# Windowed attention with its keys on the partitions and two heads in one matmul, in front of a routed expert layer

## The chip, the cores and the metric

The kernel runs on one core of one Trainium2 chip. The metric is the device time of that core in microseconds (us), taken over several runs; the profile shows one execution of the same program. A core has TensorE (matmuls, PE in the profile, with its weight loads as PEld), VectorE (DVE), ScalarE (ACT), GpSimd (POOL) and SyncE (SP, which here only issues transfers). All of the data is float32.

## The reference

Eight sequences of 576 tokens go through attention with 8 heads of 64 dimensions, in which a query sees itself and the 63 keys before it. The 512 numbers of a token then go to one of eight experts, which is chosen token by token: a token either picks the expert with its largest logit, or takes over the expert of the token before it.

```python
scores = scale * np.matmul(q, k.transpose(0, 1, 3, 2))       # scale = 1 / 8
mask = (rel >= 0) & (rel < window)                           # rel = query - key, window = 64
scores = np.where(mask, scores, -1000000000.0)
scores = scores - np.max(scores, axis=-1, keepdims=True)
attn = np.exp(scores)
attn = attn / (np.sum(attn, axis=-1, keepdims=True) + 1e-09)
x = np.matmul(attn, v)                                       # then (B, S, H * D)
...
logits = np.einsum('bsd,de->bse', x, w_gate)                 # 8 experts
local_gate = 1.0 / (1.0 + np.exp(-np.einsum('bsd,de->bse', x, w_local).squeeze(-1)))
...
h = np.maximum(x[b, s] @ w1[e], 0.0)
out[b, s] = p[e] * (h @ w2[e])                               # e: fresh argmax, or the token before's; p = softmax of logits
```

The queries, keys and values are normal random numbers times 0.1.

## The kernel before

Three functions follow one another. `attention` writes the attention's rows to DRAM (`xs`) and the nine gate columns of each token to SBUF (`lt`). `route` works out from `lt` which expert each token has, and sorts the tokens into 25 blocks of 256 places, each with one expert. `experts` takes a block at a time: it gathers 256 rows of x, transposes them (L432), multiplies with the expert's first matrix (L440, 128x256 tiles), then with its second (L452, 128x512 tiles), and scatters the rows of the output (L456). It needs the routing's result for each of its fetches, so nothing of it runs beside the attention.

`attention` walks over 36 chunks of 128 tokens, in two halves of four heads. The queries are on the partitions of a score tile. `scores` (L127) makes 128 queries against 192 keys, one head a matmul; two heads lie on the two halves of the 128 partitions, so that each matmul uses 64 rows of TensorE. VectorE scales and adds the mask (L137; L133 in the chunks that have no chunk before them), finds the row maximum (L141), and ScalarE takes the exponential head by head with that maximum as bias and the row's sum as a second output (L149). `values` needs the weights with the keys on the partitions, so it turns them with TensorE: four transposes for the chunk's own keys (`own`, L161), four for the 64 keys before (`bef`, L168), which VectorE (L163) and ScalarE (L170) copy out of PSUM. Then each head has one matmul with 64 columns for its own keys (L177), and one with 64 rows and 64 columns for the keys before (L181). `rows` divides by the sums (L190) and sends the chunk to `xs`; `logits` transposes the chunk again (L199), copies it (L201) and makes the nine gate columns (L204).

The order of the instructions on each engine is fixed when the program is built: a scheduler places them, roughly in the order of the loop (scores of a half, then the values of the half before it, then the logits of the chunk before), and each engine runs its own list in order, waiting at semaphores. The loads of q, k and v come from SyncE's queue (L114 to L116), two groups of 1152 tokens ahead at most.

A float32 matmul is two instructions in the profile, each with its own weight load; a transpose is one. So 288 matmuls at L127 stand as 576.

## Time and profile before

| what | value |
|---|---|
| runs of the kernel before | 1394.6 us median of three; 1388.53, 1394.6, 1434.29 |
| the profiled execution | span 1410.9 us, 13404 instructions; no other time of it is given |
| attention, up to the last gate column (626.8 us) | TensorE busy 616.90 of 619.80 us, mean granted clock 0.54 |
| routing and the first block's fetch (626.8 to 700.0 us) | TensorE busy 37.99 of 73.20 us |
| experts (700.0 to 1408.0 us) | TensorE busy 705.45 of 708.00 us, granted clock 1.00 |
| TensorE, VectorE, ScalarE, GpSimd in all | busy 1360.3, 332.0, 261.5 and 134.5 us |
| moved by transfers | 166.04 MB |

A matmul's duration in the profile includes the time in the pipeline, so a stream of matmuls is read by its rate (the busy time of a group over its count), not by the mean of one. Busy time says nothing of the clock: TensorE can be busy all the time at half its rate, and the granted clock beside it tells which.

### The profile page before, as it was taken

To read this page: it belongs to the slowest core of one execution; us is meant where nothing else is said; L and a number is where in the kernel's file an instruction comes from. 1 tells how busy PE (TensorE), PEld (TensorE's weight loads), DVE (VectorE), ACT (ScalarE), POOL (GpSimd) and SP (SyncE) were. 2 spreads that over 40 slices of the span, in tenths; PEclk is the share of its full clock that TensorE was granted. 3 is DMA by queue.
4 is the path that set the end of the run, shared out by engine and by line. 5 is a ranking of instruction groups with operands and counts; after the bars stand their busy time and mean duration, and the time that the engine had idled before them with its cause. 6 is when DMAs were issued, how large, how long until landed. Compare 5 with 4: busy or idle time off the path is not lost. (4 is left out here: it accounts for less than half of the span.)

```text
span 1410.9 us, 13404 instructions
## 1 busy us (share of the span) xinstructions
PE 1360.3 (96%) x5322; PEld 1001.3 (71%) x5322; DVE 332.0 (24%) x688; ACT 261.5 (19%) x828; POOL 134.5 (10%) x222
## 2 busy tenths in 40 slices
PE   7999999999999999976499999999999999999998
PEld 5888788887888788865366677667766776667665
DVE  3533333233333334348110011001110011001100
ACT  3432332232232234220011111111101110111011
POOL 1000000000000000000201111111111111111100
PEclk7855555555555557555599999999999999999999
DMA  9202300033000000000745454545354545454520
GB/s 348 85 15 105 127 15 16 8 105 127 15 15 15 16 15 24 15 16 20 293 143 200 156 202 147 217 157 215 141 217 157 208 151 208 166 186 172 192 74 0
DMA packets 35678, 166.04 MB, mean 118 GB/s; under 512 B 4493, under 2 KB 16797, under 8 KB 29216
## 3 DMA queue, kind: packets, MB, share of 16 engines
q1 hardware_dynamic: 24672, 133.17, 25.8%
q0 software_dynamic: 10944, 32.02, 5.9%
q8 instruction: 42, 0.69, 0.2%
q14 instruction: 20, 0.16, 0.0%
HBM read 146.29 MB, written 22.55 MB: 120 GB/s over the span
## 5 line engine op out<-in xcount | busy, mean ns | idle before, releaser
L440 PE MATMUL hp<-xt,w 128*128 128x256 f32 x1600 | 352.0, 381 | 0.0
L452 PE MATMUL yp<-w,h 128*128 128x512 f32 x800 | 347.5, 592 | 0.0
L440 PEld LDWEIGHTS hp<-xt,w 128*128 128x128 f32 x1600 | 305.9, 191 | 52.2 <-issue 11.5
L452 PEld LDWEIGHTS yp<-w,h 128*128 128x128 f32 x800 | 150.3, 190 | 179.5 <-issue 179.4
L443 DVE TENSOR_SCALAR h<-hp 128x256 f32<-128x256 f32 x100 | 42.5, 425 | 631.0 <-issue 360.7
L127 PE MATMUL sp<-kt,qt 64*128 64x192 f32 (+1 forms) x576 | 179.6, 553 | 8.2 <-DMA kt<-in_k_dram 8.0
L177 PEld LDWEIGHTS xo<-vt,owns 128*128 128x128 f32 x576 | 120.7, 310 | 23.8 <-issue 21.3
L127 PEld LDWEIGHTS sp<-kt,qt 64*128 64x128 f32 x576 | 100.1, 297 | 50.7 <-issue 45.5
L149 ACT ACTIVATE e<-s,nmax 128x192 f32<-128x192 f32 (+1 forms) x288 | 125.5, 438 | 41.9 <-DVE nmax L141 41.4
L177 PE MATMUL xo<-vt,owns 128*128 128x64 f32 x576 | 131.3, 404 | 0.0
L181 PE MATMUL xo<-vt,befs 64*128 64x64 f32 x512 | 116.7, 402 | 0.0
L181 PEld LDWEIGHTS xo<-vt,befs 64*128 64x128 f32 x512 | 109.2, 309 | 7.0 <-issue 3.5
L455 ACT ACTIVATE y<-yp,pw 128x512 f32<-128x512 f32 x50 | 34.4, 687 | 380.2 <-PE yp L452 380.2
L445 ACT ACTIVATE h<-hp 128x256 f32<-128x256 f32 x100 | 38.3, 383 | 325.1 <-PE hp L440 325.1
L161 PE MATMUL own<-ident,e 128*128 128x128 f32 x288 | 90.7, 418 | 0.0
L137 DVE SCALAR_TENSOR_TENSOR s<-sp,mask 128x768 f32<-128x768 f32 x64 | 61.0, 954 | 124.4 <-PE sp L127 124.2
L170 ACT COPY befs<-bef 64x512 f32<-64x512 f32 x64 | 37.1, 580 | 275.0 <-PE bef L168 274.9
L456 POOL DMA_INDIRECT out_dram<-y,idx x50 | 50.4, 1009 | 366.2 <-ACT y L455 358.9
L163 DVE COPY owns<-own 128x512 f32<-128x512 f32 x72 | 49.7, 691 | 124.9 <-PE own L161 123.2
L418 POOL DMA_INDIRECT xg<-xs,idx x50 | 48.7, 973 | 318.2 <-PE tp L432 268.0
L168 PE MATMUL bef<-ident,e 128*128 128x128 f32 x256 | 75.7, 409 | 0.0
L161 PEld LDWEIGHTS own<-ident,e 128*128 128x128 f32 x288 | 54.5, 214 | 27.0 <-issue 17.0
(118 smaller groups left out, 647.6 us busy)
## 6 DMA issues: line engine op xcount, KB each, us to landing
w<-in_w_dram SPq DMA_DIRECT2D x50, 2048.0 KB, 8.8
qt<-in_q_dram SPq DMA_DIRECT2D x12, 768.0 KB, 9.1
kt<-in_k_dram SPq DMA_DIRECT2D x12, 768.0 KB, 10.5
vt<-in_v_dram SPq DMA_DIRECT2D x12, 768.0 KB, 11.6
xs<-x POOLq DMA_DIRECT2D x36, 256.0 KB, 2.3
xg<-xs,idx POOLq DMA_INDIRECT x50, 8.1
out_dram<-y,idx POOLq DMA_INDIRECT x50, 2.8
wgs<-in_wg_dram POOLq DMA_DIRECT2D x1, 18.0 KB, 4.5
```

The costliest lines, as they stand in the source:

```text
L127: nc.tensor.matmul(sp[:, j, i * KW + lo:(i + 1) * KW], lhsT=qt[h, 2 * half + i, t0:t0 + P], rhs=kt[h, 2 * half + i, t0 - WIN + lo:t0 + P], ...
L137: nc.vector.scalar_tensor_tensor(s.rearrange("p j i k -> p j (i k)"), sp[:, :, :2 * KW], DH ** -0.5, m.rearrange("p (o x) -> p o x", o=1). ...
L149: nc.scalar.activation(e[:, o + lo:o + KW], s[:, j, i, lo:], Act.Exp, bias=nmax[:, j, i:i + 1], accum_out=st["sum"][:, h:h + 1])
L161: nc.tensor.transpose(own[:, s, :], e[:, o:o + P], ident)
L163: nc.vector.tensor_copy(owns, own)
L168: nc.tensor.transpose(bef[:, s, :], e[:, s * KW:s * KW + P], ident)
L177: nc.tensor.matmul(st["xo"][:, head(s)], lhsT=owns[:, s, :], rhs=vt[:, c, head(s)], start=(half == 0 and s == 0), stop=bool(st["lo"]), ski ...
L181: nc.tensor.matmul(st["xo"][:, head(s)], lhsT=befs[WIN:, s, :], rhs=vt[WIN:, c - 1, head(s)], start=False, stop=True, skip_group_check=True)
L418: nc.gpsimd.indirect_dma_start(out=x, out_offset=None, in_=xs[:, :], in_offset=bass.IndirectOffsetOnAxis(ap=idx[:, n * BC + i:n * BC + i + ...
L440: nc.tensor.matmul(hp, lhsT=st["w1"][:, kk, m * P:(m + 1) * P], rhs=st["xt"][:, kk, :], start=(kk == 0), stop=(kk == DK - 1))
L452: nc.tensor.matmul(yp, lhsT=st["h"][:, m, i * P:(i + 1) * P], rhs=st["w2"][:, m, :], start=(m == 0), stop=(m == FK - 1))
L456: nc.gpsimd.indirect_dma_start(out=out[:, :], out_offset=bass.IndirectOffsetOnAxis(ap=idx[:, s:s + 1], axis=0), in_=y, in_offset=None, bou ...
```

## The change

The attention is written anew. It walks over 9 stretches of 512 tokens and, in each, over 4 pairs of heads: 36 units. The host lays k and v out as block-diagonal 128x128 tiles, one for each 64 keys and each pair of heads, so that one matmul with 128 rows serves both heads: the score tile then has 2 x 64 keys on its partitions and 128 queries (the keys' own block and the next) in its columns. `scores` is eight such matmuls and one exponential over 1024 columns straight from PSUM, with no maximum taken off; a multiplication with a mask of zeros and ones follows on VectorE. The weights have their keys on the partitions already, so `values` multiplies them with the block-diagonal v as they are, eight matmuls and one more for the last block of the stretch before, into x with its head dimensions on the partitions. GpSimd adds up the two halves of the weights that a query has (`t`). `gates` makes from x and `t`, in one PSUM tile, the nine gate columns of every pair of heads and the row sums (a selection matrix of ones, `sel`): eight matmuls with 32 rows of output and 512 columns. `rows` transposes that tile (four) and x (sixteen), divides by the sums, adds the heads' gate columns up, and sends the rows to `xs`.

The transposes of the weights, the mask's addition, the row maxima and the separate transposes for the logits are gone. The loads of k and v double, because of the zeros in the blocks. Since no maximum is taken off, the program looks afterwards whether all row sums lie between 1e-20 and 1e20 (`f`, `ok`, `flag`); where one doesn't, the old attention (`careful`), the routing and the experts run once more behind a branch at the program's end.

```diff
+SC = 4 * P
+NSC = N // SC
+HP = H // 2
+KB = SC // WIN
+SB = S // WIN
+GW = 32
...
-    attention(tc, q, k, v, xs, lt, wgs, ident)
+    ok = const.tile([P, 1], F32, name="ok")
+    wg2s = const.tile([P, HP, GW], F32, name="wg2s")
+    nc.gpsimd.dma_start(out=wg2s, in_=wg2)
+    attention(tc, q, k2, v2, xs, lt, ok, wg2s, ident)
+    bad = const.tile([1, 1], I32, name="bad")
+    flag(tc, ok, bad, ident)
     route(tc, lt, idx, pw, ej, ident)
     experts(tc, xs, w1, w2, out, idx, pw, ej, ident)
+    b = nc.values_load(bad[0:1, 0:1], min_val=0, max_val=1,
+                       skip_runtime_bounds_check_because="the result of a comparison")
+    with tc.If(b > 0):
+        careful(tc, q, k, v, xs, lt, wgs, ident)
+        route(tc, lt, idx, pw, ej, ident)
+        experts(tc, xs, w1, w2, out, idx, pw, ej, ident)
...
-def attention(ctx, tc, q, k, v, xs, lt, wgs, ident):
-    """Softmax over the window for each chunk of 128 tokens, then its rows of x and its logits.
...
+def flag(ctx, tc, ok, bad, ident):
...
+    op = ps.tile([1, P], F32, name="op")
+    nc.tensor.transpose(op, ok, ident)
+    lo = fp.tile([1, 1], F32, name="lo")
+    nc.vector.tensor_reduce(lo, op, axis=AX.X, op=Alu.min)
+    nc.vector.tensor_scalar(bad, lo, 0.5, None, Alu.is_lt)
...
+def attention(ctx, tc, q, k2, v2, xs, lt, ok, wg2, ident):
...
-    ld = ctx.enter_context(tc.tile_pool(name="at_load", bufs=2))
+    qp = ctx.enter_context(tc.tile_pool(name="at_q", bufs=2))
+    pp = ctx.enter_context(tc.tile_pool(name="at_p", bufs=HP + 3))
...
     ps_s = ctx.enter_context(tc.tile_pool(name="at_ps_s", bufs=2, space=PSUM))
-    ps_t = ctx.enter_context(tc.tile_pool(name="at_ps_t", bufs=2, space=PSUM))
     ps_x = ctx.enter_context(tc.tile_pool(name="at_ps_x", bufs=1, space=PSUM))
...
+    mask = cp.tile([P, 2 * KB, 2 * WIN], F32, name="mask")
+    nc.vector.tensor_scalar(mask[:, :, :WIN], colf, rowf, None, Alu.is_ge)
+    nc.vector.tensor_scalar(mask[:, :, WIN:], colf, rowf, None, Alu.is_lt)
+    nc.vector.memset(mask[:, KB - 1, WIN:], 0.0)
...
+    sel = cp.tile([P, GW], F32, name="sel")
+    nc.vector.memset(sel, 0.0)
+    for i in range(2):
+        nc.vector.memset(sel[i * WIN:(i + 1) * WIN, 2 * (E + 1) + i:2 * (E + 1) + i + 1], 1.0)
...
+    def load(sc):
+        t0 = sc * SC
+        n = min(SC + WIN, N - t0)
+        qt = qts[sc] = qp.tile([P, HP, SC + WIN], F32, name="qt")
+        kt = kts[sc] = qp.tile([P, HP, KB, P], F32, name="kt")
+        vt = vts[sc] = qp.tile([P, HP, KB, P], F32, name="vt", bufs=3)
+        step = 1 if sc == 0 else HP
+        for i in range(0, HP, step):
+            h = slice(i, i + step)
+            nc.sync.dma_start(out=qt[:, h, :n], in_=q[:, h, t0:t0 + n])
+            nc.sync.dma_start(out=kt[:, h], in_=k2[sc, :, h])
+            nc.sync.dma_start(out=vt[:, h], in_=v2[sc, :, h])
...
+    def scores(sc, hp):
+        qt, kt = qts[sc], kts[sc]
+        sp = ps_s.tile([P, KB, 2 * WIN], F32, name="sp")
+        for j in range(KB):
+            n = 2 * WIN if sc * KB + j + 1 < N // WIN else WIN
+            nc.tensor.matmul(sp[:, j, :n], lhsT=kt[:, hp, j, :],
+                             rhs=qt[:, hp, j * WIN:j * WIN + n], start=True, stop=True)
+        p = pp.tile([P, KB, 2 * WIN], F32, name="p")
+        m = (KB - sc if sc else KB)
+        full = KB if (sc + 1) * SC < N else KB - 1
+        for a, b, w in ((0, full, 2 * WIN), (full, KB, WIN)):
+            if a < b:
+                nc.scalar.activation(p[:, a:b, :w], sp[:, a:b, :w], Act.Exp, scale=DH ** -0.5)
+                nc.vector.tensor_tensor(p[:, a:b, :w], p[:, a:b, :w], mask[:, m + a:m + b, :w], op=Alu.mult)
+        return p
...
+    def values(sc, hp, p, t, xt):
+        vt = vts[sc]
+        before = last.get(hp)
+        xp = ps_x.tile([P, SC], F32, name="xp")
+        if before is not None:
+            nc.tensor.matmul(xp[:, :WIN], lhsT=vts[sc - 1][:, hp, KB - 1, :], rhs=before[:, KB - 1, WIN:],
+                             start=True, stop=False, skip_group_check=True)
+        for j in range(KB):
+            n = 2 * WIN if j + 1 < KB else WIN
+            nc.tensor.matmul(xp[:, j * WIN:j * WIN + n], lhsT=vt[:, hp, j, :], rhs=p[:, j, :n],
+                             start=(before is None and j == 0), stop=(j == KB - 1), skip_group_check=True)
+        nc.gpsimd.tensor_tensor(t[:, hp, WIN:].rearrange("p (b q) -> p b q", q=WIN), p[:, 1:, :WIN],
+                                p[:, :KB - 1, WIN:], op=Alu.add)
+        if before is not None:
+            nc.gpsimd.tensor_tensor(t[:, hp, :WIN], p[:, 0, :WIN], before[:, KB - 1, WIN:], op=Alu.add)
+        else:
+            nc.gpsimd.tensor_copy(t[:, hp, :WIN], p[:, 0, :WIN])
+        nc.scalar.copy(xt[:, hp, :], xp)
+        last[hp] = p
+    def gates(sc, t, xt):
+        gp = ps_x.tile([P, SC], F32, name="gp")
+        for hp in range(HP):
+            g = gp[hp * GW:(hp + 1) * GW, :]
+            nc.tensor.matmul(g, lhsT=wg2[:, hp, :], rhs=xt[:, hp, :], start=True, stop=False, skip_group_check=True)
+        for hp in range(HP):
+            g = gp[hp * GW:(hp + 1) * GW, :]
+            nc.tensor.matmul(g, lhsT=sel, rhs=t[:, hp, :], start=False, stop=True, skip_group_check=True)
+        gs = wk.tile([P, SC], F32, name="gs")
+        nc.vector.tensor_copy(gs, gp)
+        return gs
+    def rows(sc, xt, gs):
+        gt = ps_x.tile([P, 4, HP, GW], F32, name="gt")
+        for c in range(4):
+            nc.tensor.transpose(gt[:, c].rearrange("p h g -> p (h g)"), gs[:, c * P:(c + 1) * P], ident)
+        su = allsum[:, sc].rearrange("p c (h j) -> p c h j", j=2)
+        nc.vector.tensor_copy(su, gt[:, :, :, 2 * (E + 1):2 * (E + 1) + 2])
+        r = wk.tile([P, 4, H], F32, name="r")
+        nc.vector.tensor_scalar(r, allsum[:, sc], 1e-9, None, Alu.add)
+        nc.vector.reciprocal(r, r)
+        for c in range(4):
+            n = sc * 4 + c
+            g = wk.tile([P, HP, 2, E + 1], F32, name="g")
+            rc = r[:, c, :]
+            nc.vector.tensor_tensor(g, gt[:, c, :, :2 * (E + 1)].rearrange("p h (j e) -> p h j e", j=2),
+                                    rc.rearrange("p (h j o) -> p h j o", j=2, o=1).to_broadcast([P, HP, 2, E + 1]),
+                                    op=Alu.mult)
+            nc.vector.tensor_reduce(lt[:, n, :], g.rearrange("p h j e -> p e (h j)"), axis=AX.X, op=Alu.add)
+            xr = ps_x.tile([P, H, DH], F32, name="xr")
+            for hp in range(HP):
+                nc.tensor.transpose(xr[:, 2 * hp:2 * hp + 2, :].rearrange("p h d -> p (h d)"),
+                                    xt[:, hp, c * P:(c + 1) * P], ident)
+            x = wk.tile([P, H, DH], F32, name="x")
+            nc.vector.tensor_tensor(x, xr, rc.rearrange("p (h o) -> p h o", o=1).to_broadcast([P, H, DH]), op=Alu.mult)
+            nc.gpsimd.dma_start(out=xs[n * P:(n + 1) * P, :], in_=x.rearrange("p h d -> p (h d)"))
...
+    load(0)
+    load(1)
+    units = [(sc, hp) for sc in range(NSC) for hp in range(HP)]
+    ps = {units[0]: scores(*units[0])}
+    done = None
+    for i, (sc, hp) in enumerate(units):
+        if hp == 0:
+            t = wk.tile([P, HP, SC], F32, name="t")
+            xt = wk.tile([P, HP, SC], F32, name="xt")
+        if i + 1 < len(units):
+            ps[units[i + 1]] = scores(*units[i + 1])
+        values(sc, hp, ps.pop((sc, hp)), t, xt)
+        if hp == 0 and 1 <= sc < NSC - 1:
+            load(sc + 1)
+        if hp == 1 and done:
+            rows(*done)
+        if hp == 0 and done:
+            done = done[0], done[2], gates(*done)
+        if hp == HP - 1:
+            done = sc, t, xt
+    rows(sc, xt, gates(*done))
...
+    fl = allsum.rearrange("p a b c -> p (a b c)")
+    f = wk.tile([P, NSC * 4 * H], F32, name="f")
+    nc.vector.tensor_scalar(f, fl, 1e20, None, Alu.is_le)
+    nc.vector.scalar_tensor_tensor(f, fl, 1e-20, f, Alu.is_ge, Alu.mult)
+    nc.vector.tensor_reduce(ok, f, axis=AX.X, op=Alu.min)
...
+@with_exitstack
...
-    nc.vector.tensor_scalar(idx, tab[:, 0, :], float(N), None, Alu.add)
+    at = tl("at", P, NS)
+    nc.vector.tensor_scalar(at, tab[:, 0, :], float(N), 0.0, Alu.add, Alu.max)
+    nc.vector.tensor_scalar(idx, at, float(N), None, Alu.min)
...
+    wg2 = _np.zeros((2, DH, HP, GW), wg.dtype)
+    for j in range(2):
+        wg2[j, :, :, j * (E + 1):(j + 1) * (E + 1)] = wg.reshape(HP, 2, DH, E + 1)[:, j].transpose(1, 0, 2)
+    def diagonal(a, keys_first):
+        a = a.transpose(0, 2, 1, 3).reshape(NSC, KB, WIN, HP, 2, DH)
+        d = _np.zeros((NSC, 2, WIN, HP, KB, 2, WIN), a.dtype)
+        for j in range(2):
+            d[:, j, :, :, :, j, :] = a[:, :, :, :, j].transpose(*((0, 2, 3, 1, 4) if keys_first else (0, 4, 3, 1, 2)))
+        return d.reshape(NSC, P, HP, KB, P)
```

The order of the instructions shows three places on which the prediction rests. First, TensorE in the middle of the attention. Before, one half of a chunk (`sp` are the scores, `own` and `bef` the transposed weights, `xo` the values, `xp` and `lp` the logits):

```order
L127 MATMUL sp<-kt,qt 128x192
L181 MATMUL xo<-vt,befs 128x64 x4
L168 MATMUL bef<-ident,e 128x128 x4
L127 MATMUL sp<-kt,qt 128x192 x3
L177 MATMUL xo<-vt,owns 128x64 x4
L181 MATMUL xo<-vt,befs 128x64 x4
L199 MATMUL xp<-ident,x 128x128 x4
L161 MATMUL own<-ident,e 128x128 x2
```

Now, from the end of one stretch's gates on (`gt` the transposed gates, `xr` the transposed x, `sp` scores, `xp` values; 36 such units in all):

```order
L220 MATMUL gt<-ident,gs 128x128 x4
L236 MATMUL xr<-ident,xt 128x128 x4
L172 MATMUL sp<-qt,kt 128x128 x7
L236 MATMUL xr<-ident,xt 128x128 x4
L172 MATMUL sp<-qt,kt 128x128
L188 MATMUL xp<-p,vt 128x64
L192 MATMUL xp<-p,vt 128x128 x3
L236 MATMUL xr<-ident,xt 128x128 x4
L192 MATMUL xp<-p,vt 128x128 x4
L192 MATMUL xp<-p,vt 128x64
L172 MATMUL sp<-qt,kt 128x128 x4
```

The transposes of the weights are gone; each unit is now eight score matmuls and nine value matmuls with all 128 rows, and the transposes of x (`xr`, one PSUM buffer) stand between them in groups of four.

Second, VectorE at the same place. Before, by half chunk (`s` is the masked score, `nmax` the row maximum, `owns` the copied transposes):

```order
L137 SCALAR_TENSOR_TENSOR s<-sp,mask_93 128x768
L141 TENSOR_REDUCE nmax<-s 128x4
L163 COPY owns<-own 128x512
L190 TENSOR_TENSOR x<-xo,r 128x512
L137 SCALAR_TENSOR_TENSOR s<-sp,mask_93 128x768
L187 TENSOR_SCALAR r<-sum 128x8
L141 TENSOR_REDUCE nmax<-s 128x4
```

Now, over one stretch, from the copy of the gates on (`p` is the mask's multiplication):

```order
L214 COPY gs<-gp 128x512
L180 TENSOR_TENSOR p<-p,mask 128x1024
L222 COPY allsum<-gt 128x32
L224 TENSOR_SCALAR r<-allsum 128x32
L225 RECIPROCAL r<-r 128x32
L230 TENSOR_TENSOR g<-gt,r 128x72
L239 TENSOR_TENSOR x<-xr,r 128x512
L233 TENSOR_REDUCE lt<-g 128x9
L230 TENSOR_TENSOR g<-gt,r 128x72 x2
L233 TENSOR_REDUCE lt<-g 128x9 x2
L230 TENSOR_TENSOR g<-gt,r 128x72
L239 TENSOR_TENSOR x<-xr,r 128x512
```

Four multiplications of 1024 columns a stretch take the place of the masks and maxima, and the divisions of x stand between them: the third group of `xr` can only be written when the second has been read by VectorE.

Third, the end of TensorE's list. Before and now:

```order
L432 MATMUL tp<-ident,xg 128x128 x8
L452 MATMUL yp<-w_6134,h 128x512 x16
L440 MATMUL hp<-xt,w_6233 128x256 x32
L452 MATMUL yp<-w_6235,h 128x512 x16
L496 UNCONDITIONAL_BRANCH
```

```order
L651 MATMUL yp<-w_4337,h 128x512 x16
L639 MATMUL hp<-xt,w_4436 128x256 x32
L651 MATMUL yp<-w_4438,h 128x512 x16
L88 TENSOR_LOAD bad
L90 COMPARE_AND_BRANCH
```

The experts' matmuls are the same; behind them every engine now loads the flag and branches on it.

More of the change, by code (lines that the diff above doesn't have):

```diff
@@ L88, in attention @@
     ps_x = ctx.enter_context(tc.tile_pool(name="at_ps_x", bufs=1, space=PSUM))
+    row = cp.tile([P, 1], I32, name="row")
+    nc.gpsimd.iota(row, pattern=[[0, 1]], base=0, channel_multiplier=1)
+    nc.vector.tensor_scalar(row, row, WIN - 1, None, Alu.bitwise_and)
+    rowf = cp.tile([P, 1], F32, name="rowf")
+    nc.vector.tensor_copy(rowf, row)
+    col = cp.tile([P, 2 * KB, WIN], I32, name="col")
+    nc.gpsimd.iota(col, pattern=[[0, 2 * KB], [1, WIN]], base=0, channel_multiplier=0)
+    colf = cp.tile([P, 2 * KB, WIN], F32, name="colf")
@@ new lines, in attention @@
+    last = {}
+    def scores(sc, hp):
[13 more added lines that the diff above has]
+        return p
@@ new lines, in attention, with careful @@
+    rows(sc, xt, gates(*done))
[4 more added lines that the diff above has]
+    nc.vector.tensor_reduce(ok, f, axis=AX.X, op=Alu.min)
+@with_exitstack
+def careful(ctx, tc, q, k, v, xs, lt, wgs, ident):
+    nc = tc.nc
+    cp = ctx.enter_context(tc.tile_pool(name="ca_const", bufs=1))
+    ld = ctx.enter_context(tc.tile_pool(name="ca_load", bufs=2))
+    wk = ctx.enter_context(tc.tile_pool(name="ca_work", bufs=3))
+    ps_s = ctx.enter_context(tc.tile_pool(name="ca_ps_s", bufs=2, space=PSUM))
+    ps_t = ctx.enter_context(tc.tile_pool(name="ca_ps_t", bufs=2, space=PSUM))
+    ps_x = ctx.enter_context(tc.tile_pool(name="ca_ps_x", bufs=1, space=PSUM))
```

23 lines of the change are left out of this document (18 added, 5 removed).

## The prediction

> **What bounds the kernel now.** I read the page's shares and slices first, then the stretches of the three functions, then single matmul groups, then TensorE's list around the places where its clock changed.
>
> ```profile
> span 1410.9 us, 13404 instructions
> PE 1360.3 (96%) x5322; PEld 1001.3 (71%) x5322; DVE 332.0 (24%) x688; ACT 261.5 (19%) x828; POOL 134.5 (10%) x222
> PE   7999999999999999976499999999999999999998
> PEclk7855555555555557555599999999999999999999
> ```
>
> TensorE is busy nearly everywhere, but in the first 17 slices mostly at half its clock. The stretches (length; busy time and count of PE, PEld, DVE, ACT, POOL; clock; DMA share; GB/s):
>
> ```profile
> 7.00:626.80 619.80, 616.90 (x2640) 501.23 (x2640) 220.60 (x382) 187.14 (x676) 30.21 (x106) 0.54 0.17 59
> 626.80:700.00 73.20, 37.99 (x119) 28.37 (x120) 38.85 (x160) 0.83 (x2) 9.57 (x10) 0.50 0.38 151
> 700.00:1408.00 708.00, 705.45 (x2565) 471.73 (x2563) 72.03 (x146) 72.29 (x149) 89.54 (x90) 1.00 0.45 165
> ```
>
> So the attention is 619.8 us of TensorE at clock 0.54, with VectorE at 220.6 and ScalarE at 187.1 far behind. What comes after it, 1410.9 - 626.8 = 784.1 us, is routing and experts, which the change leaves as they are.
>
> Why is the clock low while the engine has no idle time? The weight of a matmul and its columns both take time. Full-clock rows, from the experts:
>
> ```profile
> L440 PE MATMUL hp<-xt,w 128*128 128x256 f32 x1600 | 352.0, 381 | 0.0
> L452 PE MATMUL yp<-w,h 128*128 128x512 f32 x800 | 347.5, 592 | 0.0
> 823.10 1.04 PE L432 MATMUL tp<-ident,xg 128*128 128x128 f32 x8
> 823.98 1.45 PE L452 MATMUL yp<-w,h 128*128 128x512 f32 x3
> ```
>
> 352.0/1600 = 0.220 us for 256 columns, 347.5/800 = 0.434 for 512: 0.85 ns a column, weights hidden. Eight 128-column transposes start 0.88 us ahead of the next group: 0.110 each, weight load included. And the half-clock rows, from the place where the clock rose at 532.7:
>
> ```profile
> 525.45 1.01 PE L127 MATMUL sp<-kt,qt 64*128 64x192 f32 x4
> 526.39 0.69 PE L161 MATMUL own<-ident,e 128*128 128x128 f32 x2
> 527.01 1.97 PE L181 MATMUL xo<-vt,befs 64*128 64x64 f32 x8
> 528.90 0.69 PE L161 MATMUL own<-ident,e 128*128 128x128 f32 x2
> 529.39 1.06 PE L168 MATMUL bef<-ident,e 128*128 128x128 f32 x4
> 530.37 1.01 PE L127 MATMUL sp<-kt,qt 64*128 64x192 f32 x4
> 531.32 1.11 PE L199 MATMUL xp<-ident,x 128*128 128x128 f32 x4
> ...
> 525.90:529.30 3.40, 3.40 (x16) 2.52 (x15) 1.25 (x2) 0.00 (x0) 0.00 (x0) 0.50 0.00 0
> 529.30:532.70 3.40, 3.40 (x16) 2.30 (x16) 1.86 (x3) 2.14 (x8) 0.69 (x2) 0.50 0.15 57
> 532.70:536.10 3.40, 3.40 (x30) 3.04 (x28) 2.26 (x3) 1.77 (x7) 0.00 (x0) 1.00 0.08 25
> ```
>
> At half clock a column takes 1.7 ns. The eight value matmuls at 527.01 are 0.24 us apart (1.89/8), of which 64 columns stream 0.11; the rest waits for weights. Counted so, columns stream in some 0.55 of the stretch before 529.3 (scores 0.5, transposes 0.8, values half of their time and on half of the rows), and in some 0.8 of 529.3 to 532.7, where eight transposes of 0.22 and the scores follow each other; behind that one the clock is 1.00. Busy is 3.40 of 3.40 in all three. I read this as: the clock rises after a stretch of 3.4 us with columns in about 0.8 of it, and then bears the same mix at about 0.5 for a while. The Trainium skill (TensorE: Matmul & The Clock Gate, Part 1) says that about 3.4 us of sustained activity release the clock and that gaps of over 3 us lose it. If that were busy time, the clock would be full before and after alike, and the rival of half clock below would have no chance; the trace doesn't agree, busy throughout at 0.50, so that rival stays.
>
> **The change, part by part.** *TensorE.* All new matmuls of the units have 128 rows and, but for a few, 128 columns. Scores: 36 x 8 = 288, twice as instructions, 576. Values: 36 x 8 + 32 = 320, so 640. At 0.110 (the row at 823.10: same weight, same columns) these are 1216 x 0.110 = 133.8 us. Bounds: 0.109 if only columns count (128 x 0.85), 0.218 if weights hid behind nothing. I take the transposes' rate, where weights and columns alternate just so. Transposes: 9 x (4 + 16) = 180 x 0.110 = 19.8 us. Gates: 9 x 8 matmuls of 512 columns, 144 instructions; one after the other 144 x 0.434 = 62.5 us. But they write four separate groups of 32 output rows. No quarter of the array occurs in the trace, halves do:
>
> ```profile
> 10.27 3.01 PE L127 MATMUL sp<-kt,qt 64*128 64x192 f32 x16 [0.17 <-DVE s L133]
> ```
>
> Sixteen of 192 columns at half clock would be 16 x 192 x 1.7 ns = 5.2 us in a row; they took 3.01, so two run at a time. I take four at a time for the gates, 36 x 0.434 = 15.6 us, because of this row, and keep 62.5 for the range. The Trainium skill (TensorE: Matmul & The Clock Gate, Part 3) says that matmuls with up to 32 output rows, put on different groups of 32 output partitions, run concurrently; by it the 15.6 would hold, and no row here shows it. Sum: 133.8 + 19.8 + 15.6 = 169.2 us at full clock.
>
> *The clock.* In a unit, columns of 0.109 stream in every 0.110 at either clock, against 0.8 at which it rose. So I expect 1.00 from about 6 us after the first score on (cost of the start at half: 3 us), and the 0.85 or so that remains with waits holds it.
>
> *What lies beside TensorE.* Nearest rows, mean ns of one:
>
> ```profile
> L149 ACT ACTIVATE e<-s,nmax 128x192 f32<-128x192 f32 x256 | 113.1, 444 | 22.4 <-DVE nmax L141 21.8
> L149 ACT ACTIVATE e<-s,nmax 128x128 f32<-128x128 f32 x32 | 12.4, 390 | 19.6 <-DVE nmax L141 19.6
> L201 ACT COPY xt<-xp 128x512 f32<-128x512 f32 x36 | 21.1, 585 | 118.4 <-PE xp L199 118.3
> L137 DVE SCALAR_TENSOR_TENSOR s<-sp,mask 128x768 f32<-128x768 f32 x64 | 61.0, 954 | 124.4 <-PE sp L127 124.2
> L190 DVE TENSOR_TENSOR x<-xo,r 128x512 f32<-128x512 f32 x36 | 24.9, 692 | 50.7 <-PE xo L181 42.1 <-PE xo L177 8.5
> L95 POOL TENSOR_SCALAR_AFFINE_SELECT mask<-mask 128x384 f32<-128x384 f32 x2 | 1.0, 520 | 0.0
> ```
>
> ScalarE's slope is 54 ns for 64 columns, so an exponential of 1024 is 444 + 832 x 0.84 = 1.14 us; with the copy of x 1.73 a unit. VectorE: (954 - 692)/256 = 1.02 ns a column, so the mask's multiplication is 1.22 us; a stretch has four, the copy of the gates (0.69), four divisions (0.69), and some dozen of small ones at 0.2 or so: about 11 us. GpSimd's addition of 448 + 64 columns is 0.7 us by L95, which has one input; with two perhaps twice that. TensorE has 169.2/9 = 18.8 us a stretch: it stays the bound. Within a unit, the chain from the end of the scores to the values is 1.14 + 1.22 + some 0.3; meanwhile TensorE does the unit before's values and the next one's scores, 34 x 0.110 = 3.7 us. So 1.0 us is to spare, and that cover is thin. What shows: the x transposes have one PSUM buffer. Between the second and the third group TensorE has 0.9 us of work, VectorE 2.1 us in its list (reductions and divisions). I charge 1.5 to 2.5 us a stretch, 18 in all.
>
> *Loads.* 512 tokens now bring 1.18 MB of q, 2.1 of k and of v: 48.4 MB, with 9.4 MB of x. The first loads of before ran at
>
> ```profile
> DMA packets 6957, 11.39 MB, mean 380 GB/s; under 512 B 239, under 2 KB 5159, under 8 KB 6956
> ```
>
> from 10 to 40 us. At that rate 57.8 MB are 152 us, less than TensorE's 169, and two stretches are loaded ahead. Only the start shows: stretch 1 has landed at about 30 us, when TensorE is through with stretch 0 (8 + 3 + 19); 3 us. If waits were nil, loads would be the next bound, 17 us lower.
>
> *Ends.* The first score came at 8.0 us, behind its loads:
>
> ```profile
> 8.02 2.08 PE L127 MATMUL sp<-kt,qt 64*128 64x128 f32 x16 [8.02 <-DMA kt<-in_k_dram]
> 626.79 0.45 DVE L281 TENSOR_REDUCE mx<-lt 128x36 f32<-128x288 f32 x1
> 1406.50 0.98 POOL L456 DMA_INDIRECT out_dram<-y,idx  x1 [5.88 <-ACT y L455]
> ```
>
> I keep 8. At the end of the attention nothing covers the last copy, gates, their copy, transposes, divisions and reductions: 8 us more than is counted. At the program's end each engine loads the flag and branches; the profile shows neither, and behind the last scatter at 1406.50 the span has 4.4 us, in which part of it lies. I take 2 us, bounds 0 and 10. `flag` and the clamp of `idx` are five small instructions; nil.
>
> Sum: 8 + 169.2 + 3 + 3 + 18 + 8 = 209 us to the end of the attention, against 626.8; 209 + 784.1 + 2 = 995 us. The profiled span is 16 us over the runs' median, between their lowest and highest; the attention's clock, above 0.5 in three of its slices, can account for that. I don't take it off; it widens the range downward. **Forecast: 995 us**, own range 970 to 1025.
>
> **Rivals.** *Gates one after the other*: for it, no row shows four quarters at once. 62.5 instead of 15.6: 1042. It decides if the gate group takes 6.9 us a stretch instead of 1.7.
>
> *The unit's chain shows*: the spare 1.0 us is used up by VectorE's divisions, or by GpSimd. 1.5 us a unit, 54 in all: 1049. The Trainium skill (SBUF — State Buffer, the two separate sides) says that a VectorE operation with two SBUF inputs and a GpSimd operation that reads SBUF exclude each other; the mask's multiplication and GpSimd's additions are such a pair. The trace of before has no such pair, so no row shows it.
>
> *The clock stays at half*: if the zeros in the blocks or the waits keep columns below 0.8. Then 169.2 doubles and the waits of 18 vanish: 995 + 169 - 18 = 1146; with the gates in a row 1193. Against it: the count of columns above.
>
> *The old path runs*, which is the case of slower: some row sum is outside 1e-20 to 1e20, the flag is set, and attention, routing and experts run again, 619.8 + 73.2 + 708.0 = 1401: 2396 us. One sum decides. Scores of inputs at 0.1 are near 0, so sums lie between about 1 and 64; only a column of `t` or `sel` that is not what it seems would do it.
>
> **How the numbers follow.** Forecast 0.55; gates in a row 0.17, the chain 0.13, and both of these 1096, in their shares; half clock 0.12; old path 0.02; 0.01 for no gain at all. The range from 965 to 1100 holds the first three, 0.85, less the edges. What a measurement of this kernel can tell from no change is about 2%, 28 us, as its runs lie 1388 to 1434. All but two of the cases are far below: faster 0.97, same 0.01, slower 0.02.
>
> **What would show it.** The granted clock is 1.00 from some 15 us on to the end of the attention; scores and values stand at 0.11 us an instruction; the gate group takes 1.7 us; the last gate column is there near 209 us; the stretch from there to the end is 784 us as before. It is wrong if the clock shows 0.5 there, if TensorE waits for `p` by more than 1 us in each unit, or if lines of `careful` show instructions.

## The result, and the profile after

The kernel after takes 1019.1 us in the median of four runs (1018.22 to 1021.96). The kernel before, beside it, took 1414.4 (four runs, 1388.53 to 1434.29). The ratio is 0.732, 95% interval 0.729 to 0.735; it leaves out disturbed runs of the kernel before, so it isn't the quotient of the two medians. The profiled execution took 1018.22 us, 1.7 more than its span. The forecast was 995 us with a range of 965 to 1100: the sign and the range held, and the time is 24 us above the forecast.

The page of after, with the rows that answer to those of before:

```profile
span 1016.5 us, 10264 instructions
PE 940.1 (92%) x4223; PEld 671.2 (66%) x4223; DVE 213.9 (21%) x519; ACT 132.2 (13%) x228; POOL 180.7 (18%) x226
PE   7998888974659999999999999999999999999996
PEclk9999898995559999999999999999999999999998
```

By the profile's clock row TensorE is near full clock from the first slice on, and the long row of 5s of before is left only in the three slices of the routing. The row doesn't show the very start: the first 16 scores, at 5.69 us, take 3.76 us, about twice the 1.84 us that 16 take later, so TensorE begins at half rate here too. And two 8s stand among the 9s of the attention (the first nine slices), and TensorE's own row shows 8s in the same place. The stretches (length; busy time and count of PE, PEld, DVE, ACT, POOL; clock; DMA share; GB/s):

```profile
8.00:229.50 221.50, 195.10 (x1532) 169.32 (x1531) 99.69 (x200) 57.74 (x76) 77.37 (x114) 0.95 0.63 252
229.50:303.00 73.50, 38.15 (x123) 28.70 (x124) 39.03 (x165) 0.83 (x2) 10.14 (x11) 0.51 0.38 154
303.00:1011.00 708.00, 704.55 (x2561) 470.88 (x2559) 71.99 (x146) 72.39 (x149) 89.56 (x90) 1.00 0.44 165
```

The attention ends at 229.5 us (626.8 before, forecast 209). The rest is 1016.5 - 229.5 = 787.0 us (784.1 before, forecast 786.1). So of the 23 us between the sum and the profiled execution 20 lie inside the attention, 0.9 behind it, and 1.7 outside the span.

Where the attention has them is in the waits and in the clock beside them. The waits of after, from its start to 260 us (engine, what waited, line, what for: us in total, times, longest):

```profile
DVE x L239 <- DMA xs<-x: 38.8, 7, 7.9
...
PE xp L192 <- DVE p L180: 14.9, 5, 4.1
...
PE xr L236 <- DVE x L239: 8.3, 11, 2.1
...
PE sp L172 <- DMA kt<-in_k_dram: 6.8, 2, 5.7
```

TensorE waits five times for `p`, for 2.0 to 4.1 us. Five times in 36 units is not the unit's chain, so the question is what these five have in common. VectorE's list and then TensorE's, around one of them (start, us, line, operation, count, idle time before it and what ended it):

```profile
125.09 0.69 DVE L239 TENSOR_TENSOR x<-xr,r 128x512 f32<-128x512 f32 x1 [6.97 <-DMA xs<-x]
125.70 2.35 DVE L180 TENSOR_TENSOR p<-p,mask 128x1024 f32<-128x1024 f32 x2
```

```profile
121.63 2.00 PE L172 MATMUL sp<-qt,kt 128*128 128x128 f32 x16
123.47 0.33 PE L188 MATMUL xp<-p,vt 128*128 128x64 f32 x2
126.97 3.43 PE L192 MATMUL xp<-p,vt 128*128 128x128 f32 x16 [3.16 <-DVE p L180]
130.33 1.21 PE L209 MATMUL gp<-xt,wg2s 128*32 128x512 f32 x8
131.37 1.03 PE L212 MATMUL gp<-t,sel 128*32 128x512 f32 x8
132.33 2.05 PE L172 MATMUL sp<-qt,kt 128*128 128x128 f32 x16
```

`x`, the divided rows of a chunk, has two buffers, and its fourth write of a stretch waits until the second has landed in `xs`. VectorE runs its list in order, so for 6.97 us the mask's multiplications of two units stand behind that division, TensorE runs out of work, and the 16 values at 126.97 are followed by the next group only after 3.36 us, where the 16 scores at 121.63 are after 1.84: half clock. In the issues of transfers (queue, kind, count, size, median us from issue to landing) the writes of before, over its attention from 30 to 620 us, stand as

```profile
xs<-x POOLq DMA_DIRECT2D x34, 256.0 KB, 2.3
```

and those of after, from 30 to 220 us, as

```profile
xs<-x POOLq DMA_DIRECT2D x32, 256.0 KB, 7.0
```

The clock follows the hole. The stretches of 3.4 us around two such waits (columns as above, the clock third from the end):

```profile
96.54:99.96 3.42, 0.89 (x9) 0.76 (x7) 1.29 (x2) 1.02 (x1) 0.29 (x1) 1.00 0.97 412
99.96:103.37 3.41, 2.82 (x13) 2.82 (x14) 1.67 (x2) 0.00 (x0) 2.97 (x4) 0.50 1.04 442
103.37:106.79 3.42, 3.42 (x21) 1.27 (x20) 0.00 (x0) 0.59 (x1) 0.90 (x2) 0.50 0.64 267
106.79:110.20 3.41, 3.41 (x34) 2.91 (x27) 0.69 (x1) 0.77 (x1) 0.00 (x0) 1.00 0.00 0
...
123.85:127.27 3.42, 0.30 (x2) 0.31 (x3) 2.18 (x3) 0.90 (x1) 0.75 (x2) 1.00 1.05 441
127.27:130.68 3.41, 3.41 (x20) 3.14 (x22) 0.78 (x1) 0.19 (x1) 3.41 (x4) 0.50 0.95 399
130.68:134.10 3.42, 3.42 (x31) 2.02 (x24) 0.69 (x1) 0.39 (x1) 0.00 (x0) 1.00 0.41 170
```

A stretch in which TensorE is busy for 0.89 or 0.30 us runs at full clock, and the next one at half. The first of the two costs two such stretches, since 2.82 of 3.41 us weren't enough to bring the clock back, the second costs one. One of the five waits costs no clock at all: its 1.99 us, up to 77.14, fall across the border of two stretches, which keep 2.50 and 2.34 us of work (72.65 to 76.06 and 76.06 to 79.48 us), and the clock stays at 1.00. Behind the other four lie four pieces at half clock, with 18.07 us of TensorE's work in them (6.24 + 3.41 + 5.01 + 3.41), which at full clock would be 9.0.

So the theory with which the experiments began: (A) the writes of `x` land three times as late because the loads of the doubled k and v run beside them, two buffers are too few for that, and the holes cost 15 us of waiting and 9 us of clock. The rivals: (B) the unit's own chain (exponential, mask, GpSimd's additions) is what makes TensorE wait for `p`, and the wait for the write lies beside it; (C) the writes are late because GpSimd's queue is slow, whatever the loads do.

### The profile page after: what moved, and what is told of

Its sections match the earlier page's. It is cut to its first block, busy times and chain, and to the rows that moved or that the text cites. A ratio compares the mean times of both kernels' runs of the same rounds, so it can differ in the third digit from the quotient of the medians.

```text
span 1016.5 us, 10264 instructions
## 1 busy us (share of the span) xinstructions
PE 940.1 (92%) x4223; PEld 671.2 (66%) x4223; DVE 213.9 (21%) x519; ACT 132.2 (13%) x228; POOL 180.7 (18%) x226
## 5 line engine op out<-in xcount | busy, mean ns | idle before, releaser
L192 PE MATMUL xp<-p,vt 128*128 128x128 f32 (+1 forms) x576 | 77.8, 290 | 15.1 <-DVE p L180 14.9
L192 PEld LDWEIGHTS xp<-p,vt 128*128 128x128 f32 x576 | 73.8, 206 | 16.8 <-DVE p L180 15.6
L172 PE MATMUL sp<-qt,kt 128*128 128x128 f32 x576 | 77.5, 286 | 6.8 <-DMA kt<-in_k_dram 6.8
L172 PEld LDWEIGHTS sp<-qt,kt 128*128 128x128 f32 x576 | 71.7, 200 | 13.3 <-issue 13.3
L195 POOL TENSOR_TENSOR t<-p 128x448 f32<-128x448 f32 x36 | 45.0, 1251 | 66.8 <-DVE p L180 66.7
L180 DVE TENSOR_TENSOR p<-p,mask 128x1024 f32<-128x1024 f32 (+2 forms) x40 | 45.0, 1141 | 42.5 <-ACT p L179 42.5
L631 PE MATMUL tp<-ident,xg 128*128 128x128 f32 x200 | 29.4, 291 | 21.6 <-DMA xg<-xs,idx 21.6
L179 ACT ACTIVATE p<-sp 128x1024 f32<-128x1024 f32 (+2 forms) x40 | 36.9, 933 | 90.4 <-PE sp L172 70.3
L631 PEld LDWEIGHTS tp<-ident,xg 128*128 128x128 f32 x200 | 24.9, 150 | 25.9 <-issue 20.9
L632 DVE COPY xt<-tp 128x512 f32<-128x512 f32 x50 | 32.4, 686 | 19.0 <-PE tp L631 18.7
```

What stands on the lines that cost most here:

```text
L172: nc.tensor.matmul(sp[:, j, :n], lhsT=kt[:, hp, j, :], rhs=qt[:, hp, j * WIN:j * WIN + n], start=True, stop=True)
L179: nc.scalar.activation(p[:, a:b, :w], sp[:, a:b, :w], Act.Exp, scale=DH ** -0.5)
L180: nc.vector.tensor_tensor(p[:, a:b, :w], p[:, a:b, :w], mask[:, m + a:m + b, :w], op=Alu.mult)
L192: nc.tensor.matmul(xp[:, j * WIN:j * WIN + n], lhsT=vt[:, hp, j, :], rhs=p[:, j, :n], start=(before is None and j == 0), stop=(j == KB - 1 ...
L195: nc.gpsimd.tensor_tensor(t[:, hp, WIN:].rearrange("p (b q) -> p b q", q=WIN), p[:, 1:, :WIN], p[:, :KB - 1, WIN:], op=Alu.add)
L631: nc.tensor.transpose(tp[:, kk, :], st["x"][i][:, kk * P:(kk + 1) * P], ident)
```

## Experiments

### Eight buffers for the rows of x

```diff
-            x = wk.tile([P, H, DH], F32, name="x")
+            x = wk.tile([P, H, DH], F32, name="x", bufs=8)
```

> The changed kernel with eight instead of two buffers for the divided rows x; all else as it is. Theory A (the sends of x to DRAM land late, 7 us instead of 2.3, while the loads of k and v run; with two buffers VectorE stands at the next division until one has landed, the mask's multiplications queue behind it, TensorE waits 3 to 4 us for p and loses its full clock for one or two windows): VectorE's 38.8 us of waits for xs<-x are gone, TensorE's 14.9 us of waits for p shrink to under 3, the granted clock is 1.00 from 15 us on to the end of the attention, and the last gate column is there at about 205 us instead of 229.5; the time is 990 to 998. Theory B (p is late because the mask's multiplication and GpSimd's additions hold each other up, or because exponential and multiplication are simply too long): the waits for p stay, 1014 to 1021.

Measured: 994.02 us (four runs, 992.55 to 994.64; ratio to before 0.709, 0.702 to 0.715), 25 less than after. The attention's end is the first row of VectorE's list that reads the gate columns; here it and the stretch up to it, and TensorE's waits:

```profile
206.45 0.43 DVE L478 TENSOR_REDUCE mx<-lt 128x36 f32<-128x288 f32 x1
```

```profile
8.00:206.40 198.40, 186.85 (x1532) 163.78 (x1530) 100.35 (x199) 57.74 (x76) 73.76 (x115) 0.99 0.70 282
```

```profile
PE sp L172 <- DMA kt<-in_k_dram: 7.4, 2, 5.6
PE xr L236 <- DVE x L239: 6.9, 10, 2.1
PE gt L220 <- DVE gs L214: 1.1, 2, 0.5
PE xp L192 <- ACT xt L201: 0.2, 1, 0.2
```

No wait for `p` is left, and TensorE's idle time in the attention falls from 221.50 - 195.10 = 26.4 us to 198.40 - 186.85 = 11.6. (Of the 7.4 us for `kt`, 5.6 lie ahead of the first score and outside this stretch.) With the 9.0 us of clock that makes 23.8, and the attention ends 23.1 earlier; TensorE's busy time itself falls by 8.3 us. The writes still land late, in 6.0 us (median, from 30 to 195 us), but nothing waits for them any more. B falls: the chain is as it was, and TensorE waits for it nowhere.

### The loads taken away

```diff
     def load(sc):
+        if sc >= 2:
+            qts[sc], kts[sc], vts[sc] = qts[sc - 2], kts[sc - 2], vts[sc - 2]
+            return
         t0 = sc * SC
```

> The changed kernel, two buffers for x as it is, but q, k and v are loaded for the first two stretches only; the other seven use those again (so its output is that of other data). Theory A: without loads the sends of x land in 2.3 us, nobody waits for them, and the attention ends as early as with eight buffers, about 203 us; time 988 to 998. If two buffers alone are too few whatever the traffic, or if the multiplications are the cause (theory B), waits of VectorE for xs<-x or of TensorE for p stay above 20 and 10 us and the time is over 1010.

Measured: 992.2 us (two runs, 990.29 and 994.11), with `x` at two buffers. Its writes and its stretch:

```profile
xs<-x POOLq DMA_DIRECT2D x32, 256.0 KB, 2.3
```

```profile
8.00:200.00 192.00, 180.94 (x1528) 159.99 (x1527) 99.02 (x190) 57.94 (x76) 71.18 (x110) 0.99 0.24 94
```

Without the traffic (94 GB/s instead of 252) the writes land in 2.3 us as in the kernel before, two buffers are enough, and 27 us are gone. VectorE waits for a write once, for 0.5 us, TensorE never for `p`, and the last gate column is there at 202.0 us. C falls: the queue is the same. The two experiments together say that it is the traffic that makes the landing late and the two buffers that make the late landing cost anything.

### The kernel before, with more columns in its value matmuls

The forecast's largest step was that the old attention was slow by its clock and not by its amount of work. This is the kernel before with one edit, which doubles the columns of 1088 of its instructions and nothing else:

```diff
+        def pair(s):
+            o = head(s).start // P * P
+            return slice(o, o + P)
...
-            nc.tensor.matmul(st["xo"][:, head(s)], lhsT=owns[:, s, :], rhs=vt[:, c, head(s)],
+            nc.tensor.matmul(st["xo"][:, pair(s)], lhsT=owns[:, s, :], rhs=vt[:, c, pair(s)],
...
-                nc.tensor.matmul(st["xo"][:, head(s)], lhsT=befs[WIN:, s, :], rhs=vt[WIN:, c - 1, head(s)],
+                nc.tensor.matmul(st["xo"][:, pair(s)], lhsT=befs[WIN:, s, :], rhs=vt[WIN:, c - 1, pair(s)],
```

> The kernel before with more work: each value matmul multiplies the 128 columns of two heads of v where it had the 64 of one, so that its columns fill the time that its weight load takes anyway (the sums of the two heads run into each other, so the rows of x are others). Theory C (TensorE's clock follows the share of time in which columns stream; the attention before is slow mainly because its value matmuls stream half of the time): columns stream in over 0.8 of most windows, the granted clock in the attention goes from 0.54 to above 0.85, and the attention from 620 us to between 330 and 420; time 1090 to 1200 although it does more. Rival D (the clock follows busy time, or gaps between groups, or the 64-row matmuls alone): the clock stays near 0.5 and the time at 1388 to 1440.

Measured: 1155.87 us (four runs, 1152.64 to 1160.88), ratio to before 0.824 (0.815 to 0.833). Its attention and the two value groups:

```profile
7.00:372.00 365.00, 359.99 (x2629) 300.84 (x2630) 208.31 (x370) 189.58 (x675) 29.51 (x104) 1.00 0.28 100
```

```profile
L181 PE MATMUL xo<-vt,owns 128*128 128x128 f32 x576 | 84.1, 289 | 0.7 <-DVE owns L163 0.7
L185 PE MATMUL xo<-vt,befs 64*128 64x128 f32 x512 | 73.6, 284 | 0.0
```

More work and 250 us less: the attention ends at 375.4 instead of 626.8, because 128 columns stream in the time that the weights take (84.1/576 = 0.146 us an instruction, where 64 columns at half clock took 0.24), and the clock is 1.00 over the whole of it. The matmuls of 64 rows are still there, and TensorE is no busier (359.99 of 365.00 us, against 616.90 of 619.80), so rival D falls. Of the 397 us that the change takes off the attention (626.8 - 229.5) some 251 are thus the clock's, which this kernel gains in the old layout with more work; the other 146, by subtraction, are the smaller amount of work.

### No flag and no branch

```diff
-    bad = const.tile([1, 1], I32, name="bad")
-    flag(tc, ok, bad, ident)
...
-    b = nc.values_load(bad[0:1, 0:1], min_val=0, max_val=1,
-                       skip_runtime_bounds_check_because="the result of a comparison")
-    with tc.If(b > 0):
-        careful(tc, q, k, v, xs, lt, wgs, ident)
-        route(tc, lt, idx, pw, ej, ident)
-        experts(tc, xs, w1, w2, out, idx, pw, ej, ident)
```

> The changed kernel without the flag, its load on every engine, and the branch with the old path behind it; the range of the row sums is not looked at. The stretch from the last scatter's issue to the end of the span is 7.9 us now and was 4.4 before. If the branch is what made it longer: 3 to 4 us less, 1015 to 1016.5, with 4.4 at the end. If it was something else: 1018 to 1021.

Measured: 1014.3 us (four runs, 1012.07 to 1017.66), span 1010.4. The last scatter, of after and then without the branch:

```profile
1008.60 0.98 POOL L655 DMA_INDIRECT out_dram<-y,idx  x1 [5.89 <-ACT y L654]
```

```profile
1005.89 0.98 POOL L647 DMA_INDIRECT out_dram<-y,idx  x1 [5.89 <-ACT y L646]
```

Behind it lie 1016.5 - 1008.60 = 7.9 us with the branch and 1010.4 - 1005.89 = 4.5 without, as the 4.4 of before. So the branch that isn't taken costs 3.4 us at the end. The difference of the medians, 4.8 us, is a little more than the 3 to 4 expected, but the intervals of the two ratios overlap (0.717 to 0.731 against 0.729 to 0.735), so it is the trace that carries this, not the times; in the traced execution without the branch the attention, too, ends 4.4 us earlier (225.1), which the edit doesn't explain.

### GpSimd and VectorE

With the holes gone, the waits of TensorE for `xr` are what is left inside the stretches. Behind them stood an odd row. GpSimd's list and VectorE's, in after, around 137 us (VectorE's with the same line from the attention's end):

```profile
136.83 1.14 POOL L195 TENSOR_TENSOR t<-p 128x448 f32<-128x448 f32 x1 [6.15 <-DVE p L180]
137.92 0.32 POOL L198 TENSOR_TENSOR t<-p 128x64 f32<-128x64 f32 x1
```

```profile
137.04 0.96 DVE L224 TENSOR_SCALAR r<-allsum 128x32 f32<-128x32 f32 x1
...
222.31 0.18 DVE L224 TENSOR_SCALAR r<-allsum 128x32 f32<-128x32 f32 x1
```

The addition of 1e-9 to 32 row sums takes 0.96 us there, ends when GpSimd's addition ends, and takes 0.18 us in the last stretch, where GpSimd adds nothing. Every division, and so every `xr`, is behind it. The next kernel has eight buffers of `x` and no additions on GpSimd (`t` is a constant tile of ones):

```diff
-        nc.gpsimd.tensor_tensor(t[:, hp, WIN:].rearrange("p (b q) -> p b q", q=WIN), p[:, 1:, :WIN],
-                                p[:, :KB - 1, WIN:], op=Alu.add)
...
+    t = cp.tile([P, HP, SC], F32, name="t")
+    nc.vector.memset(t, 1.0)
...
```

> The kernel with eight buffers for x, without GpSimd's additions: the tile t is filled with ones once, so that the row sums are constants (another output). Theory E (GpSimd's additions and VectorE's work on SBUF exclude each other: VectorE's r + 1e-9 over 32 columns takes 0.75 us on the mean where 0.18 is its time without an addition beside it, and the transposes of x wait for that): that instruction takes 0.2 us, the mask's multiplication falls from 1.265 to 1.20 to 1.25, TensorE's 6.9 us of waits for x shrink by 3 to 5; time 988 to 992 against 994.0. If the exclusion hides behind TensorE: 993 to 995, with the durations shorter all the same.

Measured: 988.74 us (four runs, 987.66 to 989.12), 5.3 less than with eight buffers alone. That run was on another chip; the one of the next section, which has the additions and was on the same chip as this, took 995.04. The row is

```profile
L218 DVE TENSOR_SCALAR r<-allsum 128x32 f32<-128x32 f32 x9 | 1.6, 181 | 0.3
```

so VectorE's add does wait for GpSimd's addition, and the additions cost about 5 us here. TensorE's waits for `xr` fall from 6.9 to 3.5 us. The mask's multiplication falls only from 1.265 to 1.225 us, and TensorE didn't wait for it before. That the small instruction alone carries the cost is what the last experiment asks.

### A second PSUM buffer for the x transposes

Eight buffers of `x`, and two for `xr`, whose room comes from the gates' two tiles sharing one:

```diff
-        gp = ps_x.tile([P, SC], F32, name="gp")
+        gp = ps_x.tile([P, SC], F32, name="gp", tag="g")
...
-        gt = ps_x.tile([P, 4, HP, GW], F32, name="gt")
+        gt = ps_x.tile([P, 4, HP, GW], F32, name="gt", tag="g")
...
-            xr = ps_x.tile([P, H, DH], F32, name="xr")
+            xr = ps_x.tile([P, H, DH], F32, name="xr", bufs=2)
```

> The kernel with eight buffers for x and with two PSUM buffers for the transposed x; the room comes from the gates and their transposes, which now share one bank. Theory F (TensorE waits between the groups of x transposes for VectorE's division, 6.9 us in all beside 7.7 of weight loads that wait too): these waits are gone, 986 to 991 against 994.0. If the wait only moves, to the gates' shared bank or to the values behind a longer VectorE list: 993 to 997.

Measured: 995.04 us (994.06 to 995.67), no gain. The wait only moved: two groups of transposes now run ahead, and the third waits for the same reciprocals (5.9 us in all instead of 6.9). That single buffer, to which the forecast charged 18 us, was not what held TensorE in these waits.

### The add of 1e-9 from PSUM

The row sums are copied from PSUM to `allsum`, and the add read that copy. Here it reads PSUM, ahead of the copy; first together with the second PSUM buffer, then alone, beside the kernel with eight buffers on the same chip:

```diff
-        nc.vector.tensor_copy(su, gt[:, :, :, 2 * (E + 1):2 * (E + 1) + 2])
         r = wk.tile([P, 4, H], F32, name="r")
-        nc.vector.tensor_scalar(r, allsum[:, sc], 1e-9, None, Alu.add)
+        nc.vector.tensor_scalar(r.rearrange("p c (h j) -> p c h j", j=2), gt[:, :, :, 2 * (E + 1):2 * (E + 1) + 2],
+                                1e-9, None, Alu.add)
+        nc.vector.tensor_copy(su, gt[:, :, :, 2 * (E + 1):2 * (E + 1) + 2])
```

> As the run with two buffers for transposed x, and r + 1e-9 is read from PSUM, not from the copied sums in SBUF. Theory E: an operation that reads PSUM doesn't need what GpSimd holds, so it takes 0.2 instead of 0.75 us, and the division behind it starts 0.5 us earlier in each stretch: 0 to 4 us less than the run with two buffers, 983 to 990. If it isn't the source but the write to SBUF that waits: 0.75 us stay, and no difference.

> The same program as the one with eight buffers of x, on the chip of the run beside it, as its measure: 994 us, attention ending at 206 to 207 us of the profiled execution, the add of 1e-9 for the reciprocals at 0.7 to 0.8 us.

> Eight buffers of x, and the add of 1e-9 reads the row sums from PSUM instead of SBUF; the x transposes keep their one PSUM buffer. Theory A (the small add is held up by GpSimd's additions when it reads SBUF, and TensorE waits behind it): the add falls from 0.75 to about 0.19 us, the waits of the x transposes fall, and some 5 us go: 989, the attention ends near 201. Theory B (the gain of the version with both edits needs the second PSUM buffer as well): the add is as short, but the transposes still wait for the one buffer: 993 to 994, the attention ends at 205 or 206.

Measured: both edits 989.48 us (four runs, 988.92 to 990.77; ratio 0.709, 0.707 to 0.711); eight buffers alone 993.91 (six runs, 991.63 to 994.42); eight buffers and the add from PSUM 989.06 (six runs, 988.21 to 989.33; ratio 0.709, 0.705 to 0.712). The groups of the last two kernels, in that order:

```profile
L224 DVE TENSOR_SCALAR r<-allsum 128x32 f32<-128x32 f32 x9 | 6.8, 752 | 0.3
```

```profile
L223 DVE TENSOR_SCALAR r<-gt 128x32 f32<-128x32 f32 x9 | 1.7, 192 | 2.4 <-PE gt L220 2.1
```

The ranges of the two don't overlap: 4.9 us by the medians, from one operand read elsewhere. TensorE's waits for `xr` fall from 6.9 to 3.2 us. The edit also takes the copy to `allsum`, 0.19 us, from ahead of the add; no run separates that share, but the kernel without additions, which keeps the copy there, gained no less. In the profiled executions the attention ends at 203.5 and 200.4 us (the first of these programs ended its attention at 206.4 in its other profiled execution, so one trace is good to some 3 us here, and the medians decide). The second PSUM buffer adds nothing to it. With eight buffers and this add the changed kernel takes 30 us less than after.

## Why the prediction was right, and where it was off

**What bounds the kernel: right.** The forecast read 619.8 us of attention at clock 0.54 as a matter of streaming columns, and not of idle time. The kernel before with wider value matmuls shows it directly: clock 1.00 and 251 us less with more columns.

**Amount of work and rates: right in the main, low for the gates.** Units were priced at 0.110 us an instruction; 16 scores take 1.84 us (121.63 to 123.47 above), 0.115. Gates were priced at 15.6 us, four at a time, 1.74 a stretch; where they stand together they take 2.00 (130.33 to 132.33, of which the first 0.35 at half clock), and one after another they would take 6.9. So the rival *gates one after the other* falls. The Trainium skill's rule (TensorE: Matmul & The Clock Gate, Part 3), that matmuls on different groups of 32 output rows run concurrently, holds here: 2.00 us, not 6.9. The row at 10.27 us by which the sum took four at a time doesn't carry that by itself: the clock row reads 1.00 there, and at full clock 16 matmuls of 192 columns would take 2.6 us in a row, less than its 3.01. The row at 525.45, at 0.50, does show an overlap: four in 0.94 us, where in a row they would take 1.3. And the gates don't stand together everywhere: with eight buffers a first pair, alone at 25.40 us, takes 0.98 us, and over all nine stretches the gates take some 22 us, by the starts of their groups, instead of 15.6. That is the largest miss among the rates.

**The rise of the clock: the runs agree with its rule.** "After a stretch of 3.4 us with columns in about 0.8 of it": 2.82 of 3.41 us busy (0.83, of which 13 instructions of 0.22 us, less the head of the first, stream some 0.77 by my count, an estimate) didn't raise it, 3.41 of 3.41 did. The start at half clock, priced at 3 us, came too: 16 scores in 3.76 us instead of 1.84, and some 18 instructions from 11.21 to 14.62 us, where the next 3.42 us hold 31.

**"The 0.85 or so that remains with waits holds it": this step failed.** The sum had the waits as small ones, 1.5 to 2.5 us a stretch, spread between transposes. The idle total was near (26.4 us against 3 + 18 + 8), by luck, since more than half of it was of another kind and came bunched: five holes of 2.0 to 4.1 us. Four of them left only 0.30 to 1.10 us of work in a stretch of 3.4 us, far below the 0.85 of the forecast, and the clock fell; stretches that kept 2.11 us and more held it. So beside 14.9 us of waiting the holes cost 9.0 us of clock, for which the sum had nothing.

**Behind it: a queue that the sum passed over.** The division's `x` and its write were in the change, with two buffers, and the sum priced the division and never its buffer. The rows for it were there: 2.3 us from issue to landing in the before trace, at 59 GB/s of traffic; that the loads would then run beside the writes followed from the prediction's own line on loads (57.8 MB at 380 GB/s are most of the attention). It asked whether loads come late, but not what their traffic does to the other transfer. Eight buffers bring 994.0 us.

That this nearly equals the forecast of 995 is partly luck: in that kernel TensorE is busy for 189.2 us (2.4 of them ahead of the 8.0 us at which the stretch above begins) where the sum has 172 (169.2 and the start), idle for 11.6 where it has 29, and its first score comes at 5.6 us instead of 8. The rates were too low, the gates' most of all, and the waits for `xr` too high: charged with 18, they are 6.9, and what was left of them was not the one PSUM buffer but a 0.18 us instruction that took 0.75.

**The end: low.** 2 us were taken for the branch, between 0 and 10; it is 3.4.

**The unit's chain: refuted as a bound, right in one part.** The two groups with eight buffers of `x`:

```profile
L180 DVE TENSOR_TENSOR p<-p,mask 128x1024 f32<-128x1024 f32 x32 | 40.5, 1265 | 59.8 <-ACT p L179 59.8
L179 ACT ACTIVATE p<-sp 128x1024 f32<-128x1024 f32 x32 | 32.8, 1025 | 78.4 <-PE sp L172 58.3 <-DVE g L230 19.4 <-issue 0.7
```

The exponential is 1.02 us (forecast 1.14), the mask's multiplication 1.26 (forecast 1.22), and TensorE never waits for `p`: the 1.0 us to spare was enough. The exclusion of GpSimd and VectorE that this rival named is real, but where it cost time was not the multiplication with two inputs. The Trainium skill (SBUF — State Buffer, the two separate sides) gives the exclusion also to VectorE operations in a mode that uses both ports, which the prediction left out. The add from SBUF, 752 ns, against 192 from PSUM agrees with that; which mode the add ran in, no trace here shows.

**Half clock and the old path: they did not come.** The clock over the attention is 0.95, and behind the experts' last scatter the span has 7.9 us, with no place for a second attention.

## What to carry to other kernels

When a change adds traffic, look at every transfer whose buffer is waited for, not only at the loads themselves: ask how long its landing takes under that traffic, and count buffers by that. On TensorE, price a hole not by its length alone but by whether it empties a 3.4 us stretch, since then the next 3 to 7 us run at half clock; and if a kernel is busy at half clock, count streaming columns before anything else. A small instruction at the head of a chain deserves a look at its own duration: here one operand read from PSUM instead of SBUF was worth 5 us.

## What the runs showed of the hardware

- A 256 KB write from GpSimd's queue landed in 7.0 us (median) beside loads in bursts of some 430 GB/s, and in 2.3 without them, from the same queue in the program that leaves the loads out.
- A VectorE instruction of 128x32 elements with one SBUF input waited for a running GpSimd addition: 0.75 us in the mean, 0.18 without it, 0.19 reading PSUM. The division, which reads `xr` from PSUM, takes 0.684 us with GpSimd's additions (eight buffers) and 0.684 without them.
- In after, by the stretches of 3.41 us to which those above belong, the clock rose after a stretch in which TensorE was busy for all of 3.41 us, and not after 2.82 of 3.41. It was lost after stretches with 0.30, 0.89, 0.92, 1.10 and 1.30 us of work, and kept after 2.11, 2.34 and 2.50. A full-clock stretch between 1.30 and 2.11 us doesn't occur. In the kernel before, busy time alone didn't do it: 616.90 of 619.80 us busy at 0.54.
- A branch that isn't taken, with its flag loaded by the engines, cost 3.4 us at the end of the program.
